# Another hand-written order for the first block of an attention and feed-forward kernel: nine runs of V-products a group instead of eleven

## The chip, the cores and the metric

The kernel runs on one core of a Trainium2 chip. Five engines matter: TensorE (PE, matrix products), ScalarE (ACT, here above all the exponential of the softmax), VectorE (DVE), GpSimd (POOL) and SyncE (SP, which issues most of the DMAs). Each engine executes its own instructions in the order in which they were written, and waits on semaphores for the others. The metric is the time of one execution on the device, in microseconds; lower is better.

## The reference

A transformer block for 2048 tokens of width 512: attention with 32 heads of width 16 that share one key and one value head, then a gated feed-forward layer of width 1792. Each half normalizes its input and adds its output to it.

```python
def _A_ref(x, wq, wk, wv, wo):
    q = (x @ wq).reshape(B, S, H, Dh).transpose(0, 2, 1, 3)
    k = x @ wk
    v = x @ wv
    scores = jnp.einsum("bhqd,bkd->bhqk", q, k) * (Dh ** -0.5)
    p = _softmax(scores, axis=-1)
    o = jnp.einsum("bhqk,bkd->bhqd", p, v)
    return o.transpose(0, 2, 1, 3).reshape(B, S, H * Dh) @ wo

def _B_ref(x, w_gate, w_up, w_down):
    return (_gelu(x @ w_gate) * (x @ w_up)) @ w_down

h = x + _A_ref(_layernorm(x), A_wq, A_wk, A_wv, A_wo)
h2 = h + _B_ref(_layernorm(h), B_w_gate, B_w_up, B_w_down)
```

## The kernel before

The queries are cut into four blocks of 512 tokens, the heads into eight groups of four, the keys into sixteen chunks of 128. For each block, group and chunk the kernel makes the scores of four heads, takes their exponential and multiplies it with the values. Work on the feed-forward layer of one block is woven into the attention of the next.

After a prologue (normalization of all tokens, keys, values, the first queries) comes the stage that the change is about: the attention of the first block, some 256 score moves long. Nothing of the feed-forward layer can run there yet. In its place TensorE projects the queries of the three later blocks, and GpSimd splits all feed-forward weights into a high and a low part (`part_weights`).

The order of TensorE's work in this stage is a string of letters, `PERIOD`, one letter a move, repeated for each of the eight groups behind a short `OPENING`:

- **s** (`pace`, `score`, `scores`): one *score pair*, that is two matmuls for two heads against one key chunk (L371), and the exponential of both results in one ScalarE instruction (L375). There are three PSUM buffers for scores: two in one pool, and every third pair uses a third one. Two score moves make one tile `p` of probabilities; there are PB = 5 such tiles. Every fourth score move also takes a step of the weight splitting and of what is owed to a finished group (the reload of its sums, reciprocals L415, the product with them L424 and its split L128, L129).
- **v** (`finish`, `weigh`): one *V-product*, the oldest pending tile of probabilities times the values of its chunk (L379, eight matmul records in the trace), added up in PSUM in `acc`. The pool holds one `acc` only. After the sixteenth chunk of a group `evacuate` has VectorE copy it to `oT` (L392), from where it goes to DRAM (L444) and back in another layout (L410).
- **p** (`visit`): up to six projection matmuls of the generator `later_q` (L220), or one of its short norm products (L258). The result of twelve such matmuls, a chunk of queries for one block, leaves by three VectorE operations: a cast to the high part (L128), the low part (L129) and the square of the high part (L243). Four chunks of a block's queries are followed by a norm product (`pqn`), from which a bound `m` is made by VectorE (L264, L265), GpSimd (L270 to L275) and VectorE again (L286).
- **n** (`norm`): the norm product alone, if the last visit ended a block's last chunk and the product hasn't been made yet. A visit that finds the norm product next takes it and ends.

A `v` with nothing pending does nothing. When 256 score pairs have been written, `pace` calls `drain`, which writes whatever `later_q` still owes, all at once. Behind the stage 23 more pairs are paced by a simple rule, `lead`, and then the dense work begins (L798; its first product is `pp`, with the attention's output weights). ScalarE, GpSimd, VectorE and SyncE follow the same written order as TensorE: each move appends its instructions to all of them.

The list before has three visits and three `n` a group, seventeen `v` for sixteen chunks, and its V-products stand in eleven runs, five of two and six of one in the steady state.

Of the kernel before, what the change touches and what calls it, by code (L numbers as in the profile page):

```python
# [33 lines left out]

OPENING = "ssspssps"

PERIOD = "psssvvssvnsspsssvvssvnssvssvssvvssspssvssvvnsssvvssvss"

RUNS = ((0, 1, 2, 3), (4, 5, 6, 7), (8, 9, 10, 11), (12, 13))

# [19 lines left out]
def kernel(  # L60
# [98 lines left out]
    def run(outer, first):  # L159
# [888 lines left out]
        with tc.manual_schedule(engines={mybir.EngineType.SP, mybir.EngineType.DVE}):  # L1048
# [46 lines left out]
            moves = {"s": pace, "p": visit, "n": norm, "v": partial(finish, 1)}  # L1095
            for move in OPENING + PERIOD * (PER // KC):
                moves[move]()
# [453 lines left out]
```

## Time and profile before

| what | value |
|---|---|
| median of 3 runs | 1399.07 us (1398.49 to 1399.08) |
| span of the profiled execution | 1401.0 us |
| TensorE busy | 1386.0 us (99%), 10438 matmuls |
| ScalarE busy | 1033.9 us (74%) |
| VectorE busy | 632.4 us (45%) |
| GpSimd busy | 233.8 us (17%), nearly all of it in the first 300 us |
| exponentials (L375) | 1024, mean 1037 ns |
| V-product matmuls (L379) | 4096, 491.0 us busy |
| score matmuls (L371) | 1984 in the trace, 387.0 us busy |

The profiled execution's own time is its span, 1401.0 us; it is one execution beside the three that were timed. Times in the profile are microseconds from the span's start. The first exponential of the stage starts at 46.4 us and the first dense product at 315.46. A row of the timeline gives start, duration, engine, line, operation and what it writes and reads, and in brackets the idle time ahead of it and what ended that. Matmuls are pipelined and their ends are modelled, so the durations of consecutive matmuls overlap; what one costs is read from the distance of two starts.

### The profile page before, as it was taken

What the parts mean: (1) busy time and instruction counts of PE and PEld (TensorE: products, weight loads), DVE (VectorE), ACT (ScalarE), POOL (GpSimd) and SP (SyncE); (2) the same over time, 40 slices, a digit from 0 to 9 for tenths busy, and PEclk for the clock granted to TensorE, in tenths of its full rate; (3) what the DMA queues carried; (4) which work ended last, traced back from release to release, by engine and by line L of the source; (5) the groups of instructions that cost most, each with busy time, mean ns of one, the idle gap of its engine ahead of it and who ended that gap; (6) DMA issues with size and microseconds to landing.
All of it is one profiled execution on the core that took longest, in us unless ns stands there. A gap on an engine that the chain in (4) does not pass through costs nothing.

```text
span 1401.0 us, 25275 instructions
## 1 busy us (share of the span) xinstructions
PE 1386.0 (99%) x10438; PEld 757.0 (54%) x10438; DVE 632.4 (45%) x1016; ACT 1033.9 (74%) x1157; POOL 233.8 (17%) x336
## 2 busy tenths in 40 slices
PE   9999999999999999999999999999999999999998
PEld 7433333325555555545555555545555555558886
DVE  7413131314354444455364444445264443546665
ACT  8799999997787777877787777777778777762000
POOL 7577766731000000000000000000000000011000
PEclk9999999999999999999999999999999999999999
DMA  4466776744232322311422323311322332233552
GB/s 162 159 208 199 237 225 207 229 171 157 79 104 75 117 103 103 118 58 58 169 92 80 133 103 102 107 61 43 141 98 103 118 103 102 97 117 121 188 207 94
DMA packets 66783, 180.32 MB, mean 129 GB/s; under 512 B 9672, under 2 KB 9672, under 8 KB 66628
## 3 DMA queue, kind: packets, MB, share of 16 engines
q1 hardware_dynamic: 55196, 143.15, 29.4%
q0 software_dynamic: 10208, 35.26, 7.7%
q8 instruction: 84, 1.38, 0.4%
q10 hardware_dynamic: 1256, 0.20, 0.1%
q14 instruction: 39, 0.32, 0.1%
HBM read 130.87 MB, written 47.45 MB: 127 GB/s over the span
## 4 chain that ended last, share of the span: by engine, by line
PE 82%; POOL 7%; DMA 5%; issue 2%; ACT 2%; DVE 1%; POOLq 0%; ACTq 0%
PE acc L379 27%; PE s L371 16%; PE pu L798 8%; PE pg L798 8%; PE pd L798 7%; DMA w_1r<-in_B_w_up_dram 4%; PE pd L828 3%; PE pg L828 3%; PE pu L828 3%; PE pp L798 2%; ACT p L375 1%; PE pq L220 1%; POOL w_1b L129 1%; PE pp L901 1%; PE pd_rest L840 1%
## 5 line engine op out<-in xcount | busy, mean ns | idle before, releaser
L375 ACT ACTIVATE p<-s 128x1024 f32<-128x1024 f32 x1024 | 959.5, 1037 | 226.4 <-PE s L371 223.7
L379 PE MATMUL acc<-p,v_sb 128*32 128x512 f32 x4096 | 491.0, 599 | 0.2 <-DVE oT L392 0.2
L371 PE MATMUL s<-qg,kaug 50*128 50x512 f32 x1984 | 387.0, 427 | 4.2 <-ACT p L375 4.1
L371 PEld LDWEIGHTS s<-qg,kaug 50*128 50x128 f32 x1984 | 168.9, 184 | 283.2 <-ACT p L375 124.4
L379 PEld LDWEIGHTS acc<-p,v_sb 128*32 128x32 f32 x4096 | 108.7, 109 | 233.3 <-issue 219.5
L798 PE MATMUL pg<-x2h,w 64*128 64x512 f32 x672 | 175.8, 392 | 0.0
L798 PE MATMUL pu<-x2h,w 64*128 64x512 f32 x672 | 174.3, 392 | 0.0
L798 PE MATMUL pd<-w,gh 64*128 64x512 f32 x624 | 122.7, 394 | 0.3
L728 DVE TENSOR_TENSOR h<-h,pd 128x512 f32<-128x512 f32 x80 | 54.9, 686 | 145.9 <-PE pd L798 145.9
L138 POOL TENSOR_SCALAR rstd<-mv 128x1 f32<-128x1 f32 x16 | 3.6, 224 | 670.5 <-DVE mv L136 670.2
L798 PEld LDWEIGHTS pg<-x2h,w 64*128 64x128 f32 x672 | 96.0, 186 | 11.1
L798 PEld LDWEIGHTS pu<-x2h,w 64*128 64x128 f32 x672 | 95.5, 186 | 11.1
L798 PE MATMUL pg<-x2l,w 64*128 64x512 f32 x336 | 100.4, 392 | 0.0
L798 PE MATMUL pu<-x2l,w 64*128 64x512 f32 x336 | 99.8, 392 | 0.0
L957 ACT ACTIVATE ga<-ga 128x512 f32<-128x512 f32 x14 | 8.8, 632 | 88.5 <-DVE ga L954 88.5
L798 PEld LDWEIGHTS pd<-w,gh 64*128 64x128 f32 x624 | 67.3, 186 | 12.6 <-DVE u L665 1.4
L392 DVE COPY oT<-acc 128x512 f32<-128x512 f32 x32 | 22.1, 690 | 110.0 <-PE acc L379 109.9
L798 PE MATMUL pd<-w,gl 64*128 64x512 f32 x312 | 70.6, 392 | 0.0
L665 DVE TENSOR_TENSOR g<-g,pg 128x512 f32<-128x512 f32 x42 | 28.8, 685 | 90.9 <-PE pg L798 90.9
L415 DVE RECIPROCAL oc<-oc 128x128 f32<-128x128 f32 x64 | 56.6, 922 | 21.4 <-DMA oc<-acc_d 17.5
L661 DVE COPY g<-pg 128x512 f32<-128x512 f32 x42 | 29.0, 692 | 72.1 <-PE pg L798 72.1
L665 DVE TENSOR_TENSOR u<-u,pu 128x512 f32<-128x512 f32 x42 | 28.8, 685 | 68.7 <-PE pu L798 68.7
(259 smaller groups left out, 1481.2 us busy)
## 6 DMA issues: line engine op xcount, KB each, us to landing
w<-w_d SPq DMA_DIRECT2D x126, 512.0 KB
w<-w_d SPq DMA_DIRECT2D x21, 1024.0 KB
qg<-q_d SPq DMA_DIRECT2D x62, 200.0 KB
q_d<-qh SPq DMA_DIRECT2D x32, 256.0 KB
acc_d<-oT SPq DMA_DIRECT2D x31, 256.0 KB
oc<-acc_d SPq DMA_DIRECT2D x124, 64.0 KB
w_d<-w_0b POOLq DMA_DIRECT2D x14, 512.0 KB, 3.8
w_d<-w_1b POOLq DMA_DIRECT2D x14, 512.0 KB, 5.1
```

Source lines behind the costliest of these rows:

```text
L129: (eng_lo or nc.vector).tensor_tensor(lo, src, hi.bitcast(F32), op=ALU.subtract)
L220: nc.tensor.matmul(pq, wt[c][:, d, :], xt[:, d, :], start=(n == 0), stop=(n == 3 * DC - 1),)
L371: nc.tensor.matmul(s[:, a, :], kaug[rows, kc * P : (kc + 1) * P], qg[rows, u, :], start=True, stop=True,)
L375: nc.scalar.activation(p[:, 2 * u : 2 * u + 2, :], s, AF.Exp, scale=SCALE)
L379: nc.tensor.matmul(acc[32 * j : 32 * j + 32, :], v_sb[:, kc, :], p[:, j, :], start=(kc == 0), stop=(kc == KC - 1), skip_group_check=True,)
L392: nc.vector.tensor_copy(oT, acc)
L415: nc.vector.reciprocal(oc[:, 1, sl], oc[:, 1, sl])
L661: nc.vector.tensor_copy(half, bank)
L665: nc.vector.tensor_tensor(half, half, bank, op=ALU.add)
L728: nc.vector.tensor_tensor(hs[b, t], hs[b, t], bank, op=ALU.add)
L798: nc.tensor.matmul(bank, lhsT[r], rhs[r], start=(k == 0), stop=(k == n - 1), skip_group_check=True,)
L828: nc.tensor.matmul(bank, lhsT, rhs, start=(i == 0), stop=(i == len(ts) - 1))
```

## The change

One line changes, the list of moves that a group repeats:

```diff
-PERIOD = "psssvvssvnsspsssvvssvvnssvssvssvvssspssvssvvnsssvvssvss"
+PERIOD = "vsssvvnssspssvsspsssvvnsssvvsssvvsssvvsssvvssspsvsssv"
```

Each list has 32 score moves and three visits. The new one has sixteen `v`, not seventeen, and two `n`, not three. It begins and ends with a `v`, so that read as a ring it has nine runs of V-products, seven of two and two of one, and its score pairs stand mostly in threes. A projection visit follows three pairs in two of its three places. The number of instructions on each engine is unchanged; what moves is their order on all of them.

Three places of the order show it. The numbers in names are block, group, chunk and half, as each name needs them, and a running number last. The first place is on TensorE, where the first group's accumulator (`acc_0_0`) gives way to the second's (`acc_0_1`). Before:

```order
L379 MATMUL acc_0_0_781<-p_13_1009,v_sb_72 32x512 x4
L379 MATMUL acc_0_0_781<-p_14_1030,v_sb_72 32x512 x4
L371 MATMUL s_17_0_1083<-qg_0_1_816,kaug_71 128x512 x2
L371 MATMUL s_17_1_1087<-qg_0_1_816,kaug_71 128x512 x2
L379 MATMUL acc_0_0_781<-p_15_1043,v_sb_72 32x512 x4
L371 MATMUL s_18_0_1108<-qg_0_1_816,kaug_71 128x512 x2
L371 MATMUL s_18_1_1112<-qg_0_1_816,kaug_71 128x512 x2
```

Behind these stand six projections and three more score pairs, and only then the first product into `acc_0_1`. The same place in the new order:

```order
L371 MATMUL s_17_0_1079<-qg_0_1_816,kaug_71 128x512 x2
L379 MATMUL acc_0_0_781<-p_14_1030,v_sb_72 32x512 x4
L371 MATMUL s_17_1_1087<-qg_0_1_816,kaug_71 128x512 x2
L371 MATMUL s_18_0_1100<-qg_0_1_816,kaug_71 128x512 x2
L371 MATMUL s_18_1_1104<-qg_0_1_816,kaug_71 128x512 x2
L379 MATMUL acc_0_0_781<-p_15_1039,v_sb_72 32x512 x4
L379 MATMUL acc_0_1_1060<-p_16_1061,v_sb_72 32x512 x4
L371 MATMUL s_19_0_1121<-qg_0_1_816,kaug_71 128x512 x2
```

The last product of one group and the first of the next are neighbours. It is so at all seven boundaries between groups of the stage.

The second place is on TensorE again, the last projections of the stage (`pq_3_3`, the last chunk of the last block's queries) and the norm product behind them (`pqn_3_0`, with `sel`). Before:

```order
L220 MATMUL pq_3_3_2954<-xT_hi_3_94,wq_lo_3_103 128x512
L371 MATMUL s_118_1_3030<-qg_0_7_2634,kaug_71 128x512 x2
L371 MATMUL s_119_0_3035<-qg_0_7_2634,kaug_71 128x512 x2
L371 MATMUL s_119_1_3039<-qg_0_7_2634,kaug_71 128x512 x2
L379 MATMUL acc_0_7_2898<-p_115_2961,v_sb_72 32x512 x4
L379 MATMUL acc_0_7_2898<-p_116_2979,v_sb_72 32x512 x4
L371 MATMUL s_120_0_3052<-qg_0_7_2634,kaug_71 128x512 x2
L371 MATMUL s_120_1_3056<-qg_0_7_2634,kaug_71 128x512 x2
L379 MATMUL acc_0_7_2898<-p_117_2996,v_sb_72 32x512 x4
L258 LDWEIGHTS sel_104
L258 MATMUL pqn_3_0_3064<-qs_3_0_2431,sel_104 32x512
```

In the new order:

```order
L220 MATMUL pq_3_3_3137<-xT_lo_3_95,wq_hi_3_99 128x512
L220 MATMUL pq_3_3_3137<-xT_hi_3_94,wq_lo_3_103 128x512
L258 LDWEIGHTS sel_104
L258 MATMUL pqn_3_0_3159<-qs_3_0_2690,sel_104 32x512
L258 LDWEIGHTS sel_104
L258 MATMUL pqn_3_0_3159<-qs_3_1_2885,sel_104 32x512
L258 LDWEIGHTS sel_104
L258 MATMUL pqn_3_0_3159<-qs_3_2_3020,sel_104 32x512
L258 LDWEIGHTS sel_104
L258 MATMUL pqn_3_0_3159<-qs_3_3_3154,sel_104 32x512
L371 MATMUL s_128_0_3195<-qg_1_0_2912,kaug_71 128x512 x2
L371 MATMUL s_128_1_3199<-qg_1_0_2912,kaug_71 128x512 x2
```

All twelve projections of `pq_3_3` and the norm product stand in one piece here, ahead of the 257th score pair (`s_128_0`), with one lone score pair ahead of them. They are what `drain` found left over. The norm product's last operand, `qs_3_3`, is made by VectorE from these very projections.

The third place is on VectorE, ahead of the copy that empties the seventh group's accumulator (`oT_0_6`). Before:

```order
L128 CAST qh_3_2_2838<-pq_3_2_2722 128x512
L129 TENSOR_TENSOR ql_3_2_2839<-pq_3_2_2722,qh_3_2_2838 128x512
L243 TENSOR_TENSOR qs_3_2_2842<-qh_3_2_2838 128x512
L415 RECIPROCAL oc_0_2_2341<-oc_0_2_2341 128x128 x4
L424 TENSOR_TENSOR oc_0_2_2341<-oc_0_2_2341 128x512
L128 CAST o_hi_0_1709<-oc_0_2_2341 128x512
L129 TENSOR_TENSOR o_lo_0_1710<-oc_0_2_2341,o_hi_0_1709 128x512
L392 COPY oT_0_6_2938<-acc_0_6_2594 128x512
```

In the new order:

```order
L415 RECIPROCAL oc_0_2_2324<-oc_0_2_2324 128x128 x4
L128 CAST qh_3_1_2881<-pq_3_1_2723 128x512
L129 TENSOR_TENSOR ql_3_1_2882<-pq_3_1_2723,qh_3_1_2881 128x512
L243 TENSOR_TENSOR qs_3_1_2885<-qh_3_1_2881 128x512
L424 TENSOR_TENSOR oc_0_2_2324<-oc_0_2_2324 128x512
L128 CAST o_hi_0_1694<-oc_0_2_2324 128x512
L129 TENSOR_TENSOR o_lo_0_1695<-oc_0_2_2324,o_hi_0_1694 128x512
L392 COPY oT_0_6_2928<-acc_0_6_2564 128x512
```

The three operations on a finished projection have moved behind the reciprocals, next to the divide and the copy. This projection's visit is the one that stands one score pair, a V-product and three score pairs ahead of the group's last product.

More of the change, by code (lines that the diff above doesn't have):

```diff
@@ L35 @@
 OPENING = "ssspssps"
-PERIOD = "psssvvssvnsspsssvvssvnssvssvssvvssspssvssvvnsssvvssvss"
+PERIOD = "vsssvvnssspssvsspsssvvnsssvvsssvvsssvvsssvvssspsvsssv"
 RUNS = ((0, 1, 2, 3), (4, 5, 6, 7), (8, 9, 10, 11), (12, 13))
```

## The prediction

> **What bounds the kernel now.** The change reorders one stage, the first block, so I read that stage alone. First the table by stretches, one row from its middle: after the columns start:end and length come busy time and instruction count of TensorE, weight loads, VectorE, ScalarE and GpSimd, then granted clock, DMA share and GB/s.
>
> ```profile
> 180.00:220.00 40.00, 40.00 (x280) 14.54 (x278) 13.36 (x17) 39.09 (x43) 29.02 (x36) 1.00 0.67 213
> ```
>
> TensorE is busy for all 40 us and ScalarE for 39.09, so shares of busy time cannot say which of them sets the pace. The list of waits between 70 and 300 us (total us, times, longest) does:
>
> ```profile
> ACT p L375 <- PE s L371: 4.1, 14, 0.9
> PE s L371 <- ACT p L375: 1.8, 4, 0.7
> PE acc L379 <- DVE oT L392: 0.2, 1, 0.2
> ```
>
> ScalarE waits for scores more often than TensorE waits for anything. The timeline (start, duration; x8 is one V-product, x4 two score pairs, x6 three, and the last L220 row here the last of a visit of six) prices TensorE's own work from start to start:
>
> ```profile
> 140.39 1.07 PE L379 MATMUL acc<-p,v_sb 128*32 128x512 f32 x8
> 141.52 0.69 DVE L392 COPY oT<-acc 128x512 f32<-128x512 f32 x1 [0.62 <-PE acc L379]
> 144.59 1.92 PE L379 MATMUL acc<-p,v_sb 128*32 128x512 f32 x16
> 146.44 0.73 PE L371 MATMUL s<-qg,kaug 50*128 50x512 f32 x4
> 147.11 1.06 PE L379 MATMUL acc<-p,v_sb 128*32 128x512 f32 x8
> 148.10 0.73 PE L371 MATMUL s<-qg,kaug 50*128 50x512 f32 x4
> 148.76 0.50 PE L220 MATMUL pq<-xT_hi,wq_hi 128*128 128x512 f32 x1
> ...
> 150.03 0.40 PE L220 MATMUL pq<-xT_hi,wq_lo 128*128 128x512 f32 x1
> 150.35 0.97 PE L371 MATMUL s<-qg,kaug 50*128 50x512 f32 x6
> 151.25 1.92 PE L379 MATMUL acc<-p,v_sb 128*32 128x512 f32 x16
> ```
>
> Two pairs cost 0.67 us until the next kind starts, three 0.90; one V-product 0.99, two 1.85; a visit 1.59. So a pair is 0.24 and a V-product 0.86, and every run adds about 0.18 (scores) or 0.13 (V). A group of the old list has 4 runs of three pairs and 10 of two (4 x 0.90 + 10 x 0.67 = 10.30 us), 5 double and 6 single V-runs (15.19) and 3 visits (4.77): 30.26 us. Against that stand the copies that end the first and the seventh group, six groups apart, and a chain of exponentials:
>
> ```profile
> 80.15 0.69 DVE L392 COPY oT<-acc 128x512 f32<-128x512 f32 x1 [8.01 <-PE acc L379]
> 263.59 0.69 DVE L392 COPY oT<-acc 128x512 f32<-128x512 f32 x1 [0.71 <-PE acc L379]
> 300.60 13.86 ACT L375 ACTIVATE p<-s 128x1024 f32<-128x1024 f32 x15 [0.49 <-PE s L371]
> L375 ACT ACTIVATE p<-s 128x1024 f32<-128x1024 f32 x1024 | 959.5, 1037 | 226.4 <-PE s L371 223.7
> ```
>
> A group takes (263.59 - 80.15) / 6 = 30.57 us, 0.3 over TensorE's own sum. ScalarE would need (13.86 - 1.04) / 14 = 0.916 us per exponential, 29.3 for 32. TensorE's instruction stream is the bound, with ScalarE 4% behind. A bubble on TensorE therefore costs its length.
>
> **The change, part by part.**
>
> *Fewer runs.* The new group has 9 runs of three pairs, 2 of two and 1 of one (0.42 us, from 285.70 and 286.12 below): 9.86; 7 double and 2 single V-runs: 14.93; 3 visits: 4.77. Sum 29.56, which is **0.70 us less** a group than 30.26. Nothing hides this; TensorE is the bound.
>
> *The group's boundary.* There is one accumulator, and VectorE's copy has to empty it. Before, 3.07 us lie between the copy's start at 141.52 and the next group's first product at 144.59, filled with scores and a visit, so the copy is free. The new list puts the last product of a group and the first of the next into one run. A place where TensorE did wait for this copy:
>
> ```profile
> 296.67 0.55 DVE L286 TENSOR_SCALAR m<-qn,mm 128x512 fp32r<-128x512 f32 x1 [18.09 <-POOL mm L275]
> 297.39 0.69 DVE L392 COPY oT<-acc 128x512 f32<-128x512 f32 x1
> 298.14 1.92 PE L379 MATMUL acc<-p,v_sb 128*32 128x512 f32 x16 [0.23 <-DVE oT L392]
> ```
>
> The copy starts 1.13 us after the last product (140.39 to 141.52), takes 0.69, and the next product follows 0.06 later (298.14 - 298.08): 1.88 from start to start where two neighbours stand 0.86 apart. So **1.02 us more** at each of seven boundaries. Queued behind the waiting product are its twin-run's end and the next three score pairs, and behind those ScalarE. Bounds: 0.2 (the wait seen above) if scores could cover it, which the order excludes; upward, VectorE being busy. That happens once: ahead of the seventh group's copy VectorE now has the three operations on a projection and then the divide's three. The latter are priced by these rows, the former by the fence on the drain:
>
> ```profile
> 139.02 0.69 DVE L424 TENSOR_TENSOR oc<-oc 128x512 f32<-128x512 f32 x1
> 140.21 0.69 DVE L129 TENSOR_TENSOR o_lo<-oc,o_hi 128x512 fp32r<-128x512 f32 x1
> ```
>
> From the visit's last projection VectorE needs 0.43 until its cast, 2.02 for cast, subtraction and square, 1.88 for the divide: 4.33. TensorE gets from there to the copy in 0.32 + 0.42 + 0.99 + 0.90 + 1.13 = 3.76. **0.6 us** once.
>
> *The score buffers.* There are three. Where TensorE ran out of them:
>
> ```profile
> 283.11 0.96 PE L371 MATMUL s<-qg,kaug 50*128 50x512 f32 x6
> 283.71 4.69 ACT L375 ACTIVATE p<-s 128x1024 f32<-128x1024 f32 x5 [0.19 <-PE s L371]
> 284.78 0.50 PE L371 MATMUL s<-qg,kaug 50*128 50x512 f32 x2 [0.72 <-ACT p L375]
> 285.70 0.49 PE L371 MATMUL s<-qg,kaug 50*128 50x512 f32 x2 [0.41 <-ACT p L375]
> 286.12 1.93 PE L379 MATMUL acc<-p,v_sb 128*32 128x512 f32 x8
> ```
>
> An exponential starts 0.60 after its scores, and a buffer is free 1.07 after its exponential starts (283.71 to 284.78). Three pairs and two V-products take TensorE 0.90 + 1.85 = 2.75 us, ScalarE 3 x 0.916 = 2.75: dead level. But the third buffer is freed 0.60 + 2 x 0.916 + 1.07 = 3.50 after the run began, and the next run wants it at 2.75 + 0.57 = 3.32. It waits 0.18, and a pair that waited alone holds TensorE for 0.42, not 0.33: 0.27 together. That pushes the next cycle back so far that it does not wait, so every second cycle pays. Of the eight cycles of three pairs with a double run or a visit behind them, four: **1.08 us a group**. Bounds: 0, if the level cycles slip past each other, and 4 x 0.41.
>
> The five probability tiles are cheap: the list now begins a sixth before the fifth-last is consumed. ScalarE reaches it 0.60 + 2 x 0.916 = 2.43 after the run's start, while that tile's product ends at 0.90 + 1.06 = 1.96. Uncovered, 0.5 us a group.
>
> So a group takes 29.56 + 1.02 + 1.08 = 31.66, that is 1.09 over 30.57; seven full groups: **+7.6 us**.
>
> *The drain.* Two visits now go to the short norm products of the second and third block's queries, which the old list gave to `n`. Two projection visits and the last norm product are thus left for the block's end, after a single score pair. What that costs:
>
> ```profile
> 150.46 0.69 DVE L128 CAST qh<-pq 128x512 fp32r<-128x512 f32 x1 [8.24 <-DMA oc<-acc_d]
> 151.19 0.69 DVE L129 TENSOR_TENSOR ql<-pq,qh 128x512 fp32r<-128x512 f32 x1
> 151.80 0.68 DVE L243 TENSOR_TENSOR qs<-qh 128x512 bf16<-128x512 f32 x1
> 276.71 0.40 PE L258 MATMUL pqn<-qs,sel 128*32 128x512 bf16 x4
> 277.04 0.73 PE L371 MATMUL s<-qg,kaug 50*128 50x512 f32 x4
> ```
>
> Twelve projections take 1.59 + 6 x 0.23 = 3.0. The norm product needs the square of what they have just finished: 2.5 us from the last projection's start at 150.03 to 152.48, plus 0.06, where the next work otherwise follows after 0.32, so 2.2 of bubble. The product itself is 0.33. From the lone pair to the next pair 5.9 us pass, and ScalarE has one exponential: 5.0 idle. Two buffer waits among the cycles there make it 5.5. The old stretch pays 0.19 + 0.49 (rows above) and
>
> ```profile
> 277.91 5.61 ACT L375 ACTIVATE p<-s 128x1024 f32<-128x1024 f32 x6 [0.21 <-PE s L371]
> 288.82 1.94 ACT L375 ACTIVATE p<-s 128x1024 f32<-128x1024 f32 x2 [0.43 <-PE s L371]
> 291.68 8.42 ACT L375 ACTIVATE p<-s 128x1024 f32<-128x1024 f32 x9 [0.92 <-PE s L371]
> 315.46 0.39 PE L798 MATMUL pp<-wo_hi,o_hi 64*128 64x512 f32 x1
> ```
>
> 2.2 in all. **+3.3 us**, between 0.5 (no bubble) and 5. The last copy sits on VectorE behind the bound's `m`, which waits for GpSimd and now for this late product; with two pairs left as cover I add 0.2. SyncE's queue (the copy's store, its reload, then the dense stage's loads) keeps its distance from the copy, so it brings nothing of its own. The first dense product, at 315.46 now, moves by the sum: 7.6 + 0.6 + 3.3 + 0.2 = **11.7 us**. From there both programs hold the same order, and TensorE is 99% busy, so nothing gives it back.
>
> The profiled execution took 1401.0 us, 1.9 over the median of 1399.07. 1401.0 + 11.7 = 1412.7, in terms of the median **1410.8 us**.
>
> **The rivals.**
>
> *Only the boundary counts.* If the level cycles never catch a buffer in use, a group costs 29.56 + 1.02 = 30.58, just as before, and the drain, the late copy and the last boundary remain: 4.1, 1403.2 us. For it: the margin is 0.18 us. Against: the buffer wait is a sum of three measured steps. Chance 0.08.
>
> *The bubbles halve the clock.* The stretches around the two waits of 0.72 and 0.41:
>
> ```profile
> 282.66:286.07 3.41, 2.28 (x18) 0.86 (x10) 0.00 (x0) 3.22 (x4) 2.59 (x5) 1.00 0.68 225
> 286.07:289.49 3.42, 3.42 (x18) 0.91 (x20) 0.00 (x0) 2.99 (x4) 2.38 (x3) 0.50 0.69 231
> ```
>
> TensorE stood still for 1.13 of 3.41 us and then ran 3.4 us at half clock, 1.7 us lost. If each boundary, with about 0.8 us of standstill, did the same: seven times 1.7 more, 1422.7 us. Against: 0.8 is less than 1.13, and only some will share a stretch with a buffer wait. Chance 0.08. The Trainium skill's page "TensorE: Matmul & The Clock Gate", section "HAM oscillation — how this bites in real kernels", gives the rule of no idle gap above about 3.4 us. By that rule these bubbles would leave the clock alone; the trace differs, since its longest gap ahead of the halved stretch is 0.72 us.
>
> *Not slower: GpSimd holds the block's end.* The copy at 297.39 follows `m`, which waited 18.09 us for GpSimd; the next block's first product at 298.14 cannot come sooner than that in either program. If the bubbles were covered, the saved runs would meet this floor and the time be 1399, chance 0.05. If GpSimd came earlier as well, eight groups times 0.70 would show: 1399.07 - 5.6 = 1393.5, chance 0.03. TensorE reaches this floor only 0.23 us early now. Against both: the bubbles' cover was moved away, and `m` now needs the drained product too.
>
> **How the numbers follow.** The forecast has 0.75, its own range 1407 to 1414: drain between 0.5 and 5, buffer waits a little either way, one halved stretch at the drain or none. The four rivals have 0.24; the rest is slower still. The range reaches down to the first rival and up by a few halved stretches: 1403 to 1416. A measurement here tells 0.2% (2.8 us) from no change. Faster 0.03, same 0.05, slower 0.92.
>
> **What would show it.** In the new profile: TensorE waiting for the copy seven times or more, 0.8 us each; copies 31.7 us apart; TensorE's waits for score buffers risen from 4 to some thirty; the norm product behind the last projections with a gap near 2 us; the first dense product near 327 us; the span after it unchanged. Copies still 30.6 apart would break the buffer term, 29.9 or less the boundary term, and a first dense product near 315 the whole argument.

## The result, and the profile after

The changed kernel took **1414.38 us** (median of four executions, 1413.68 to 1418.06) against 1399.07 before (1398.49 to 1399.19): 1.0112 times, 95% interval 1.01 to 1.0125. Beside the experiments it was timed once more on another chip: 1415.72 against 1398.96, 1.0115 (1.0098 to 1.0132). The change makes the kernel 15.3 us slower; 1410.8 had been predicted, within 1403 to 1416. One execution of a later experiment, the one on the norm products, took 2783.73 us, about twice all others; nothing here shows why, and it is left out of that experiment's numbers.

One correction first. Ahead of the prediction, the removed line of the diff was copied with one `v` too many, and the text counts seventeen `v` in the old list. The old list is `psssvvssvnsspsssvvssvnssvssvssvvssspssvssvvnsssvvssvss`: 32 score pairs, **sixteen** `v`, three visits and three `n`. A `v` with nothing pending occurs in neither list. The prediction's count of runs (5 double and 6 single) is that of the true list, so its numbers stand.

The same stretch of the table by stretches as before (length; busy time and instructions of TensorE, weight loads, VectorE, ScalarE and GpSimd; granted clock, DMA share, GB/s), after the change:

```profile
180.00:220.00 40.00, 38.29 (x256) 14.37 (x248) 11.52 (x16) 38.21 (x42) 29.09 (x33) 1.00 0.75 233
```

TensorE was busy for all of these 40 us; now it stands still for 1.7 of them. The list of waits between 70 and 300 us says for what:

```profile
PE acc L379 <- DVE oT L392: 7.3, 7, 2.4
PE s L371 <- ACT p L375: 1.6, 4, 0.4
ACT p L375 <- PE s L371: 13.8, 25, 2.6
```

Seven waits for the copy, as forecast; before the change there was one, of 0.2 us. ScalarE's waits for scores rose from 4.1 to 13.8 us. One boundary between groups in the timeline, TensorE, VectorE and ScalarE together:

```profile
143.39 1.06 PE L379 MATMUL acc<-p,v_sb 128*32 128x512 f32 x8
144.52 0.69 DVE L392 COPY oT<-acc 128x512 f32<-128x512 f32 x1 [14.58 <-PE acc L379]
...
145.27 1.06 PE L379 MATMUL acc<-p,v_sb 128*32 128x512 f32 x8 [0.81 <-DVE oT L392]
...
146.87 1.94 ACT L375 ACTIVATE p<-s 128x1024 f32<-128x1024 f32 x2 [0.98 <-PE s L371]
```

Two neighbouring products start 1.88 us apart (143.39, 145.27), the 1.88 that the prediction read off another place. ScalarE idles 0.98 us behind it. The rest of a group, on ScalarE:

```profile
167.87 6.56 ACT L375 ACTIVATE p<-s 128x1024 f32<-128x1024 f32 x7 [0.18 <-PE s L371]
174.77 2.85 ACT L375 ACTIVATE p<-s 128x1024 f32<-128x1024 f32 x3 [0.34 <-PE s L371]
178.60 1.94 ACT L375 ACTIVATE p<-s 128x1024 f32<-128x1024 f32 x2 [0.98 <-PE s L371]
```

The copies of the first, the sixth, the seventh and the eighth group, and the first dense product:

```profile
81.25 0.69 DVE L392 COPY oT<-acc 128x512 f32<-128x512 f32 x1 [2.65 <-PE acc L379]
239.47 0.69 DVE L392 COPY oT<-acc 128x512 f32<-128x512 f32 x1 [3.25 <-PE acc L379]
272.84 0.68 DVE L392 COPY oT<-acc 128x512 f32<-128x512 f32 x1
311.18 0.69 DVE L392 COPY oT<-acc 128x512 f32<-128x512 f32 x1 [1.35 <-PE acc L379]
329.45 0.40 PE L798 MATMUL pp<-wo_hi,o_hi 64*128 64x512 f32 x1
```

A group takes (239.47 - 81.25) / 5 = **31.64 us**; 31.66 was predicted, from 30.57. The sixth of these distances is longer, 33.37. The first dense product comes 14.0 us later than before (315.46), the span ends 12.1 later (1413.1 against 1401.0).

The drain: the norm product behind the twelve projections, the next score pairs and ScalarE:

```profile
304.81 0.40 PE L258 MATMUL pqn<-qs,sel 128*32 128x512 bf16 x3 [1.51 <-DVE ql L129]
305.41 0.38 PE L258 MATMUL pqn<-qs,sel 128*32 128x512 bf16 x1 [0.20 <-DVE qs L243]
305.72 1.50 PE L371 MATMUL s<-qg,kaug 50*128 50x512 f32 x6
306.49 2.86 ACT L375 ACTIVATE p<-s 128x1024 f32<-128x1024 f32 x3 [5.01 <-PE s L371]
307.35 0.26 POOL L270 TENSOR_SCALAR mm<-q,k2m 128x1 f32<-128x1 f32 x1 [12.16 <-DVE q L265]
```

ScalarE idles 5.01 us. GpSimd, for which `m` waited 18.09 us before, now waits itself, 12.16 us, for the late norm product. In this stage two stretches of the execution ran at half clock (granted clock 0.50), where the kernel before showed one; each is shown with the stretch ahead of it:

```profile
271.78:275.19 3.41, 1.61 (x14) 0.64 (x14) 1.74 (x2) 0.84 (x2) 1.92 (x3) 1.00 0.90 238
275.19:278.61 3.42, 3.42 (x20) 0.59 (x16) 0.00 (x0) 2.83 (x3) 1.49 (x2) 0.50 0.97 281
302.49:305.91 3.42, 1.71 (x10) 0.74 (x10) 2.06 (x4) 0.00 (x0) 0.00 (x0) 1.00 0.11 13
305.91:309.33 3.42, 3.42 (x16) 1.01 (x16) 1.60 (x3) 2.84 (x3) 1.35 (x4) 0.50 0.49 161
```

The first follows the wait of 2.4 us for the seventh group's copy, the second the drain's gap of 1.51.

### The profile page after: what moved, and what is told of

Its sections match the earlier page's. It is cut to its first block, busy times and chain, and to the rows that moved or that the text cites. A ratio compares the mean times of both kernels' runs of the same rounds, so it can differ in the third digit from the quotient of the medians.

```text
span 1413.1 us, 25266 instructions
## 1 busy us (share of the span) xinstructions
PE 1389.2 (98%) x10438; PEld 752.8 (53%) x10438; DVE 631.5 (45%) x1016; ACT 1034.6 (73%) x1157; POOL 231.0 (16%) x336
## 3 DMA queue, kind: packets, MB, share of 16 engines
q8 instruction: 84, 1.38, 0.4%
## 4 chain that ended last, share of the span: by engine, by line
PE 94%; ACT 2%; DVE 1%; issue 1%; DMA 1%; POOL 0%; SPq 0%; ACTq 0%; POOLq 0%; DVEq 0%
PE acc L379 33%; PE s L371 20%; PE pu L798 8%; PE pg L798 8%; PE pd L798 7%; PE pq L220 3%; PE pd L828 3%; PE pg L828 3%; PE pu L828 3%; PE pp L798 2%; ACT p L375 2%; PE pp L901 1%; PE pk L1296 1%; PE pd_rest L840 1%; PE pxt L624 0%
## 5 line engine op out<-in xcount | busy, mean ns | idle before, releaser
L798 PEld LDWEIGHTS pg<-x2h,w 64*128 64x128 f32 x672 | 94.2, 185 | 11.5
L798 PEld LDWEIGHTS pu<-x2h,w 64*128 64x128 f32 x672 | 94.1, 185 | 11.7
```

The costliest lines, as they stand in the source:

```text
L798: nc.tensor.matmul(bank, lhsT[r], rhs[r], start=(k == 0), stop=(k == n - 1), skip_group_check=True,)
```

## The experiments

The theory at this point: a group loses 1.02 us at its boundary and 1.08 to the score buffers, the drain and a late copy come on top. But the terms had been added up as if each stood alone. So besides the sum there was a second way to forecast an experiment: to walk through its order instruction by instruction with the durations of the rows (run costs of TensorE, 0.60 us from scores to exponential, 0.91 from one exponential to the next, three buffers, one accumulator, VectorE's steps in line). It differs from the sum where one wait hides another. The experiments ran on several chips, each beside the kernel before, whose median there was 1398.96 to 1401.24 us; so a measured time is compared with the kernel before beside it. The forecasts in microseconds were reckoned from 1399.1 (before) and 1414.4 (after).

**The boundary alone, in the old list.** A first repetition with one `v` less shifts all later products by one place:

```diff
+FIRST = "psssvvssvnsspsssvvssvnssvssvssvvssspssvssvvnsssvssvss"
-            for move in OPENING + PERIOD * (PER // KC):
+            for move in OPENING + FIRST + PERIOD * (PER // KC - 1):
```

> The old list with one edit: its first repetition lacks one V-product, so that every later V-product stands one place later in the list. The old structure of runs (eleven runs a group, pairs mostly in twos) stays, the three visits and the drain stay, but the last product of a group and the first of the next now stand in one double run, as in the new list. Theory (the boundary is a price by itself, the runs' number only a small gain): each of the seven boundaries costs 1.02 us, 7.1 in all, so at least 1406.2 us from a median of 1399.1; and since TensorE, once late, meets score buffers that are in use, walking through the order with the durations of the rows gives 11.5 us, so 1410.6 us. The copies that end the groups stand about 32 us apart, and TensorE waits for the copy seven times, about 0.8 us each. Rival (threes, buffers and drain are what makes the new list slow, the boundary is covered by scores): 1399, copies 30.6 apart. Measured at 1406 or above speaks for the theory, 1401 or below for the rival.

Measured: 1419.02 us (1416.34 to 1421.7) against 1400.66, 1.0134 (1.0118 to 1.0149). In its profile (this kernel's copy is L394) the same stall stands in the old structure of runs (first the timeline, then the list of waits), and a wait that neither list showed:

```profile
114.75 1.07 PE L381 MATMUL acc<-p,v_sb 128*32 128x512 f32 x8
116.63 1.06 PE L381 MATMUL acc<-p,v_sb 128*32 128x512 f32 x8 [0.81 <-DVE oT L394]
```

```profile
PE acc L381 <- DVE oT L394: 6.4, 7, 1.5
ACT p L377 <- PE acc L381: 3.7, 7, 0.5
```

The first two copies stand 32.1 us apart (83.77, 115.89 in the timeline). With runs and visits as before, this shift alone, which puts two products of different groups side by side, makes the kernel at least as slow as the whole change. The rival, that scores cover the boundary, falls; how much of the new list's loss is the boundary's, this run can't say, since the shift brings a second price: seven times ScalarE waited 0.5 us for a probability tile (second wait), which the prediction named for the tiles "uncovered" and which the new list indeed doesn't pay. It is 18.4 us over the kernel before, where 11.5 were expected; single executions go from 1416.34 at a mean clock of .998 to 1421.7 at .996, so part of the excess goes with the clock.

**The boundary covered, in the new list.**

```diff
-PERIOD = "vsssvvnssspssvsspsssvvnsssvvsssvvsssvvsssvvssspsvsssv"
+PERIOD = "sssvvvnssspssvsspsssvvnsssvvsssvvsssvvsssvvssspsvsssv"
```

> The new list with its leading V-product moved behind the three pairs that follow it, so that a group's last product stands alone and three score pairs cover the copy; all else as in the new list. The terms of the prediction, taken as a sum: seven boundaries at 1.02 us, less 0.13 us a group for the run that is one longer, and 0.2 at the end, so 6.3 us come back: 1414.4 - 6.3 = 1408.1 us, copies 30.7 apart. Rival (the terms are not independent: three pairs, a triple V-run of 2.7 us and only three score buffers make ScalarE and TensorE wait for each other in the copy's place): walking through the order with the durations of the rows, TensorE's waits for the copy fall from 7.8 us to 0.1 and its waits for score buffers rise from 9.6 to 15.7, and 0.5 us come back: 1413.9 us, copies 31.6 apart.

Measured: 1412.99 us, 1.0086 (1.0072 to 1.0099). That is 12.3 over the kernel before, the changed kernel 15.3 and 16.8, so some 3.0 to 4.4 us come back: less than the sum's 6.3, more than the walk's 0.5. Part of it goes with the clock: three of the five executions stood at .999 to 1.0, 11.6 to 12.3 over, where the changed kernel's only execution at .999 lies 13.5 over. In the profiles the first dense product, at 329.39, is where the changed kernel's is, with two halved stretches of the stage in both. The stall for the copy is gone, and the groups are as long as ever (timeline, then the list of waits):

```profile
81.74 0.69 DVE L392 COPY oT<-acc 128x512 f32<-128x512 f32 x1 [2.66 <-PE acc L379]
178.11 2.78 PE L379 MATMUL acc<-p,v_sb 128*32 128x512 f32 x24
181.36 1.03 ACT L375 ACTIVATE p<-s 128x1024 f32<-128x1024 f32 x1 [0.98 <-PE s L371]
207.78 0.69 DVE L392 COPY oT<-acc 128x512 f32<-128x512 f32 x1 [5.65 <-PE acc L379]
```

```profile
PE s L371 <- ACT p L375: 4.3, 11, 0.4
PE acc L379 <- DVE oT L392: 0.7, 1, 0.7
```

(207.78 - 81.74) / 4 = 31.51 us a group, 0.13 less than with the stall. Behind the triple run of products ScalarE idles the same 0.98 us, and TensorE's waits for score buffers went from 4 to 11. The terms are **not a sum**: take the copy's wait away and the buffers' wait comes in its place. For the group the walk had it (31.6; the sum said 30.7).

**The norm products apart.** No visit goes to a norm product, and nothing is left for the drain:

```diff
-PERIOD = "vsssvvnssspssvsspsssvvnsssvvsssvvsssvvsssvvssspsvsssv"
+PERIOD = "vsssvvnssspssvnsspsssvvsssvvsssvvsssvvsssvvnssspsvsssv"
```

> The new list with the two n moved ahead of the visits that would otherwise meet a norm product, so that no visit is spent on a short norm product and nothing is left for the block's end; runs and boundaries as in the new list, the places of two visits swap with V-runs. Theory (the drain is a price by itself, 3.3 us less what the norm products and projections cost in their new places): walking through the order gives 2.0 us back, and the stretch of 3.4 us at half clock at the drain, 1.5 to 1.7 us, goes too: 1414.4 - 3.6 = 1410.8 us; the chain of exponentials before the first dense product has no gap above 2 us. Rival (the drain was hidden behind GpSimd's bound, which the block's end waits for): 1414.4.

Measured: 1418.07 us (median of three, 1413.0 to 1418.86), 1.0123 (1.0105 to 1.0142): no gain, a miss. The profiled execution has no halved stretch but the one at its very end, and its first dense product, 325.87, is 3.6 us earlier than the changed kernel's, which had two. Two such stretches cost about 2 x 1.7 us (an estimate: 3.41 us at half clock), so with the clock set aside the drain's removal brought next to nothing. Where it went is copies on VectorE; one of them, with the product that waits for it:

```profile
145.51 1.38 DVE L128 CAST o_hi<-oc 128x512 fp32r<-128x512 f32 x1
146.92 0.69 DVE L129 TENSOR_TENSOR o_lo<-oc,o_hi 128x512 fp32r<-128x512 f32 x1
147.53 0.68 DVE L392 COPY oT<-acc 128x512 f32<-128x512 f32 x1
148.27 1.07 PE L379 MATMUL acc<-p,v_sb 128*32 128x512 f32 x8 [2.54 <-DVE oT L392]
```

Visits moved with the norm products, and now the third and the fifth group's copies, too, stand in line behind a divide (no idle time ahead of them). TensorE's waits for copies add up to 9.1 us instead of 7.3, which takes 1.8 of the 2.0 us that the walk had given back. So the experiment trades one stall for another and doesn't isolate the drain's price.

**Both undone.**

```diff
-PERIOD = "vsssvvnssspssvsspsssvvnsssvvsssvvsssvvsssvvssspsvsssv"
+PERIOD = "sssvvvnssspssvnsspsssvvsssvvsssvvsssvvsssvvnssspsvsssv"
```

> Both edits at once, the boundary covered by three pairs and the norm products ahead of the visits; what is left of the change is nine runs of V-products and score pairs mostly in threes. If the terms were a sum: 1414.4 - 6.3 - 3.6 = 1404.5 us, 5.4 above the kernel before (the score buffers' 7.6 less 0.7 saved in each of eight groups, with some of it off). Walking through the order with the durations of the rows: 3.8 us back from the order and 1.6 from the clock, 1409.0 us, with TensorE's waits for score buffers at 14.2 us. Rival (boundary and drain are the whole loss, the threes are free): 1399 or below.

Measured: 1410.47 us, 1.0073 (1.0059 to 1.0087), 9.8 over the kernel before beside it. Neither "a sum" (1404.5, 5.4 over) nor "threes are free" (no loss); the walk's 1409.0, 9.9 over, is it. Without the boundary's stall and the drain some 60% of the loss (15.3 and 16.8) remain.

**The changed kernel once more.**

> The changed kernel once more, so that it stands beside the experiments. 1.011 times the kernel before. Theory on the difference between its executions: the order costs about 12 us, the same in each, and each stretch of 3.4 us at half clock adds about 1.7; executions whose mean granted clock is .998 or .999 lie about 12 us above those of the kernel before at the same clock, those at .995 to .997 some 13.5 to 17. Rival (the spread has nothing to do with the clock): spans and clocks of single executions don't go together.

Measured: 1412.47 us at a mean clock of .999, 1415.25 at .998, 1416.19 and 1416.67 at .997; the kernel before beside it 1398.69 to 1399.16 at .999, 1400.03 and 1400.13 at .998. Time and clock go together, as the theory says; at equal clock the distance is 13.3 to 13.8 (.999) and 15.1 to 15.2 (.998), not 12.

**ScalarE at half the work.** In the first block the exponential takes one of a pair's two heads, and the V-products read that half twice:

```diff
-            nc.scalar.activation(p[:, 2 * u : 2 * u + 2, :], s, AF.Exp, scale=SCALE)
+            e = 1 if i < PER else 2
+            nc.scalar.activation(p[:, 2 * u : 2 * u + e, :], s[:, :e, :], AF.Exp, scale=SCALE)
...
-                    acc[32 * j : 32 * j + 32, :], v_sb[:, kc, :], p[:, j, :],
+                    acc[32 * j : 32 * j + 32, :], v_sb[:, kc, :], p[:, j // 2 * 2 if first else j, :],
```

> The old list, but in the first block ScalarE takes the exponential of only one of the two heads of a score pair (128x512 in place of 128x1024), and the V-products use it for both; the other half of the first block's exponentials is left out of the computation. TensorE's instructions and their order are the same. ScalarE then needs about 0.49 us a pair, not 0.92, and score buffers come free early, so that what is left is TensorE's own order. Expected by both theories: copies of the groups 30.5 us apart, as before (30.6), since the old list hardly waits for ScalarE.

> The new list with the same half of the first block's exponentials left out. Theory (the new list is slow because ScalarE, 4% behind TensorE, hands back three score buffers too late after three pairs in a row, and the boundary is paid beside it): copies 30.2 us apart, against 31.6 with all exponentials and 30.5 for the old list with half of them; the seven waits for the copy stay, 8 us together, as they are VectorE's. Rival (boundary and drain alone cost the time, the buffers nothing): copies 31.2 or more apart. Rival (the rows misjudge what a run's end costs TensorE, so that fewer runs save nothing): 30.9 or more, 0.7 above the theory.

> The new list with its leading V-product moved behind the three pairs that follow it (as in the experiment that covers the boundary), and the same half of the first block's exponentials left out. Covering the boundary brought next to nothing with all exponentials (copies 31.5 apart, 31.6 without). Theory (there the score buffers' wait took the copy's place): without ScalarE's load the cover pays, copies 29.2 us apart, 1 us less than the new list with half the exponentials. Rival (the cover never worked, the copy's price just moved to another instruction of VectorE): the same 30.2.

One execution each: 1397.40, 1404.69 and 1405.98 us, with 1398.96 for the kernel before beside them. Since these kernels leave out half of the first block's exponentials, they are no rivals of the others; they only show where the time goes. First and sixth copy of the old list, then of the new one, and first and fifth of the new one with the boundary covered:

```profile
79.47 0.69 DVE L393 COPY oT<-acc 128x512 f32<-128x512 f32 x1 [7.93 <-PE acc L380]
231.24 0.69 DVE L393 COPY oT<-acc 128x512 f32<-128x512 f32 x1 [18.34 <-PE acc L380]
```

```profile
79.17 0.69 DVE L393 COPY oT<-acc 128x512 f32<-128x512 f32 x1 [2.65 <-PE acc L380]
230.65 0.69 DVE L393 COPY oT<-acc 128x512 f32<-128x512 f32 x1 [2.55 <-PE acc L380]
```

```profile
80.00 0.69 DVE L393 COPY oT<-acc 128x512 f32<-128x512 f32 x1 [2.66 <-PE acc L380]
197.29 0.69 DVE L393 COPY oT<-acc 128x512 f32<-128x512 f32 x1 [5.78 <-PE acc L380]
...
233.80 0.98 DVE L286 TENSOR_SCALAR m<-qn,mm 128x512 fp32r<-128x512 f32 x1 [26.00 <-POOL mm L275]
234.70 0.68 DVE L393 COPY oT<-acc 128x512 f32<-128x512 f32 x1
235.43 4.90 PE L380 MATMUL acc<-p,v_sb 128*32 128x512 f32 x24 [8.65 <-DVE oT L393]
```

30.35, 30.30 and 29.32 us a group (30.5, 30.2 and 29.2 expected). With ScalarE out of the way the new list is no longer slower per group than the old, though its seven waits for the copy are still there (6.8 us), and covering the boundary is worth 1.0 us. So fewer runs do save, 1.03 us a group (30.35 to 29.32) where 0.83 was reckoned (0.70, and 0.13 for the run that is one longer). The boundary alone uses that up (30.30 against 30.35); what makes a loss of it is ScalarE at full work, which has three score pairs in hand and no more, and then a group takes 31.5 to 31.6 us with the boundary covered or not. The third run also shows the next limit. Having gained 10.7 us by the fifth copy (197.29 against 207.98 with the new list and all exponentials), TensorE then stood 8.65 us for a copy queued behind `m`, which waits for GpSimd. So GpSimd's bound, one of the rivals, is a real floor, at the sixth group's copy too; the changed kernel stays above it by the 3.25 us that VectorE stands idle ahead of that copy (row at 239.47).

**The late copy.** In the new list the third pair's divide goes one step later, behind the seventh group's copy:

```diff
+                outs.extend([[] for _ in range(b == 0 and c == 2)])
                 outs.append([divide])
```

> The new list, with the divide of the third pair of groups (the product with the reciprocals and its split into o_hi and o_lo) one step later, so that on VectorE it stands behind the seventh group's copy and not ahead of it; all else as in the new list. There TensorE waits 2.4 us for the copy, and VectorE has no idle time ahead of it. Theory (the copy is late because the divide stands ahead of it, and its o_lo, which reads two operands from SBUF, lasts 1.64 us in place of 0.69 while GpSimd is in the middle of an instruction): the copies of the sixth and seventh group stand 31.7 us apart, not 33.4, TensorE's longest wait for a copy is 0.9 us or less, and the kernel takes 1.5 us less than the new list, 1412.9. Rival (the three operations on the projection alone make it late): 32.7 apart or more.

Measured: 1413.24 us against 1401.24, 1.0079 (1.0056 to 1.0102). The timeline shows the seventh copy on time, the list of waits none above 0.8:

```profile
239.36 0.69 DVE L392 COPY oT<-acc 128x512 f32<-128x512 f32 x1 [6.71 <-PE acc L379]
271.10 0.69 DVE L392 COPY oT<-acc 128x512 f32<-128x512 f32 x1 [1.33 <-PE acc L379]
```

```profile
PE acc L379 <- DVE oT L392: 5.7, 7, 0.8
```

31.74 us, as expected, so the divide ahead of the copy made it late, and the rival falls. The kernel is 12.0 us over the kernel before, the changed one 15.3 and 16.8: it seems to gain more than the 1.5 us of the wait, some 3 to 5 us, though the intervals overlap. Both profiles of the changed kernel have a halved stretch right behind the long wait (at 275.2 and 273.7); this one has none before its last microseconds.

**Can a list gain at all?** Two runs on the old list's side: GpSimd's bound ahead of its last split, and, with the bound ahead of the last two splits, a list found by trying orders in the walk:

```diff
-                if parts is not None and n > 12 and n % 24:
+                if parts is not None and n > 12 and n % 24 and n not in (100, 124):
```

```diff
-PERIOD = "psssvvssvnsspsssvvssvnssvssvssvvssspssvssvvnsssvvssvss"
+PERIOD = "ssvvssspssvssvvsssvvssvnssvssnpssvsspsssvvsnssvvssnsvvs"
-                if parts is not None and n > 12 and n % 24:
+                if parts is not None and n > 12 and n % 24 and n not in (100, 124, 148, 172, 196, 220):
```

> The old list, with two steps of GpSimd's weight splitting moved behind the last bound: mm stands ahead of the last split on GpSimd's queue, some 4.5 us earlier. In the kernel before, TensorE's first product of the second block waits 0.23 us for a copy that stands behind the bound's m, which waits for GpSimd. Theory (the old list is bound by TensorE's own order and by the three score buffers, and GpSimd is only just late): the wait goes, 0.7 us of the order's walk with it, 1398.3 us from a median of 1399.0, no difference that a measurement can tell. Rival (GpSimd holds the block's end back by more than its one visible wait): 1396 or less.

> Another list, found by walking orders with the durations of the rows (TensorE's run costs, three score buffers with 0.60, 1.02 and 0.91 us around an exponential, one accumulator, VectorE's steps): eleven runs of V-products a group like the old one, pairs in twos and threes, the boundary covered, no norm product left for a visit, and GpSimd's bound ahead of the last two splits as in the other run. Theory (the walk holds all that decides here): a group takes 30.7 us as before, the block's end comes 2.2 us earlier, 1396.8 us. Rival (what a list may gain is lost to halved stretches or late copies, as in the new list): 1399 or more.

Measured: 1399.96 us, 0.9999 (0.999 to 1.0008), and 1400.71 us, 1.001 (1.0001 to 1.0019). The wait for the copy went and nothing came of it, as the theory had it. The walked list takes 30.7 us a group, as forecast, but misses its 1396.8: its first dense product, 313.49, is no earlier than that of the other run, 313.28. No version here that takes all exponentials beats the kernel before. Whether another order could, with three score buffers, is open.

## Why the prediction was right

The sign and the mechanism within a group held; the size came out low, 15.3 us for 11.7 by the medians. That the span was forecast as 1412.7 and is 1413.1 is partly luck: the first dense product moved by 14.0 us, and what follows it, the same order in both, took 1083.65 us (1413.1 - 329.45) where it took 1085.54 before. Among all profiles with all exponentials this rest takes 1083.65 to 1086.03. Point by point:

- **TensorE's stream is the bound, ScalarE 4% behind.** Right, and too simple. The two share one ring of three buffers. When ScalarE had half its work, a group of the new list fell by 1.34 us (31.64 to 30.30) and one of the old list by 0.22 (30.57 to 30.35).
- **Fewer runs, 0.70 less.** Borne out in kind, where ScalarE doesn't interfere: 29.32 us a group with the boundary covered and half the exponentials, against 30.35, somewhat more than priced.
- **Boundary, 1.02.** Measured 1.88 from start to start, exactly as priced; seven waits.
- **Score buffers, 1.08.** The group's sum is right to 0.02 us (31.64 against 31.66), and the pattern is there. Two successive cycles of three pairs and two products, on TensorE after the change:

```profile
158.49 1.21 PE L371 MATMUL s<-qg,kaug 50*128 50x512 f32 x6
159.63 1.92 PE L379 MATMUL acc<-p,v_sb 128*32 128x512 f32 x16
161.48 0.97 PE L371 MATMUL s<-qg,kaug 50*128 50x512 f32 x6
162.38 1.92 PE L379 MATMUL acc<-p,v_sb 128*32 128x512 f32 x16
```

  The first run of pairs takes 1.14 us until the products start, the second 0.90. In this group four runs of three, every second one, take 1.14 to 1.19 us, together some 1.1 us over 0.90 each. But boundary and buffers were added as two causes, and they are one budget. Covered, the boundary gives back 0.13 us a group and not 1.0. Had the prediction been asked what repairs the list, this step would have failed it.
- **"TensorE's waits for score buffers risen from 4 to some thirty".** Wrong as a sign to look for: four stand in the list of waits. The others show on TensorE as longer runs of pairs (rows above), not as waits in that list. In the list it is ScalarE's waits that rose, to 25 from 14.
- **Late seventh copy, 0.6.** Too small: the sixth distance is 33.37, 1.73 over the others, 1.35 in the second profile, and nothing when the divide was moved. Most of the missing microsecond is in these rows:

```profile
271.05 1.32 POOL L129 TENSOR_TENSOR w_1b<-w_1r,w_1b 128x512 fp32r<-128x512 f32 x1
271.28 1.64 DVE L129 TENSOR_TENSOR o_lo<-oc,o_hi 128x512 fp32r<-128x512 f32 x1
```

  The prediction took 0.69 us for `o_lo` from a row (140.21) where it began 0.05 us ahead of a GpSimd cast. Here it began while GpSimd was in an instruction that ended at 272.37, and ended 0.55 later (272.92). The cast `o_hi` ahead of it took 0.72 us for 0.43 (at 270.53). In the second profile it ended 0.56 after GpSimd's cast (272.52 and 271.96), and before the change 0.56 after another (262.89 and 262.33). The Trainium skill's page "SBUF — State Buffer", section "Who interferes with whom", says that a VectorE instruction with two inputs in SBUF contends with a GpSimd instruction that reads SBUF. The trace agrees: `ql`, whose first input lies in PSUM, kept its 0.69 us in the second profile (at 268.54) in the middle of a GpSimd subtraction (268.33 to 269.61).
- **Drain, 3.3.** The drain itself was right, 5.01 us of idle ScalarE for 5.0; TensorE's waits at the norm product are 1.51 + 0.20, and from the last projection's start to the next scores it takes 2.80 us (302.92 to 305.72) where 0.32 + 2.2 + 0.33 = 2.85 was priced. What was mis-sized is "the old stretch pays 2.2 in all": 0.43 and 0.92 of it stand in and right behind that execution's halved stretch. Without one (old list with GpSimd's bound early) the old stretch pays 0.21 + 0.19 + 0.19. From the seventh copy to the first dense product it takes 313.28 - 263.04 = 50.24 us there and 325.65 - 271.10 = 54.55 with the divide moved, neither with a halved stretch: 4.3, not 3.3 + 0.2.
- **The median, 3.6 us above the forecast.** The late copy's 1.1 and the drain's 0.8 are half of it: 11.7 + 1.1 + 0.8 = 13.6, close to the distance of the one execution of the changed kernel that stood at .999 (13.3 to 13.8). The rest goes with the clock, though no run holds the clock fixed. The prediction compared the profiled execution's span, 1401.0, with a median that contains 1.8 us around the span (the single executions list both), so the profiled execution of the kernel before was 3.7 us above its median, not 1.9. It had a halved stretch in the stage; the profile of the old list with GpSimd's bound early, at a mean clock of .999, has none there, and .999 is where most executions of the kernel before lie. Those of the changed kernel stood at .995 to .999. The rival "the bubbles halve the clock" was right in kind, with one or two stretches in this stage of an execution and not seven.

```profile
226.05:229.46 3.41, 0.73 (x6) 0.25 (x4) 0.00 (x0) 1.57 (x3) 3.10 (x4) 1.00 0.69 237
229.46:239.70 10.24, 4.27 (x21) 0.99 (x24) 1.58 (x2) 0.00 (x0) 8.56 (x14) 0.50 0.51 161
```

These two rows are of the run with half the exponentials and the boundary covered. In its wait of 8.65 us the clock went to half, for 10.24 us. The Trainium skill's rule that the prediction weighed ("TensorE: Matmul & The Clock Gate", section "HAM oscillation — how this bites in real kernels": no idle gap above about 3.4 us) fits this one; the stretches behind gaps of 2.41 and 1.51 us speak against it as a lower limit. A gap of this size doesn't always do it: the drain's gap is the same in the second profile of the changed kernel and with the divide moved, and no halved stretch follows there, nor behind the wait of 2.54 us in the run with the norm products apart. The busy share ahead doesn't settle it either. With the boundary covered, 3.41 us with 2.48 busy and no wait above 0.42 (217.07 to 220.48) were followed by half clock; in the second profile of the changed kernel, 3.42 us with 1.91 busy (300.93 to 304.35) were not. What decides is left open.

## What to carry to other kernels

When two engines pass work through a small ring of buffers, don't price the one engine's run costs and stalls and add them up: count what the other has in hand (here three pairs, 2.75 us) against the longest stretch in which it gets nothing new, and walk the order. A copy that empties the only accumulator belongs behind at least its own start-to-start price of other work, but covering it pays only if the cover doesn't starve the other engine. Before a stretch of one profiled execution serves as the "old cost", look whether the clock was halved in it.

## What the runs showed of the hardware beyond that

- A bubble on TensorE can cost more than its length: waits of 2.4 and 2.1 us for the seventh group's copy were followed, in the two profiles of the changed kernel, by a stretch of 3.41 us at half clock, some 1.7 us more (an estimate). With the divide moved neither the long wait nor the stretch is there. The wait of 2.54 us in another run had no such stretch behind it.
- Whether VectorE's `o_lo` lasts 0.69 or 1.64 us goes with what GpSimd is doing at that moment, here splitting feed-forward weights that this stage doesn't use. In the stage's rows of all thirteen profiles it lasted 0.97 us or more fifteen times. Fourteen of these ended 0.54 to 0.56 us after a GpSimd cast or subtraction of the splitting that ran beside it, and none of the rows with 0.69 us began inside one.
- A cast from SBUF, `o_hi`, is held as well: 0.43 us in many rows, 1.38 in the run with the norm products apart (145.51), where it ended 0.29 us after a GpSimd subtraction that was running when it began (145.01 to 146.60). The three other casts of 1.38 or 1.39 us ended 0.28 or 0.29 us after one.
